# Retention attention with a SoLU layer: late transposes moved from TensorE to DMA, second-layer output in its own PSUM banks, more load buffers

## The chip, the core and the metric

The kernel runs on one core of a Trainium2 chip. The metric is the time of one execution on the device in microseconds (us). The engines that compute are TensorE (PE; its weight loads are shown as PEld), VectorE (DVE), ScalarE (ACT) and GpSimd (POOL); SyncE (SP) issues most of the transfers, which sixteen DMA engines carry out. SBUF is the working memory with 128 partitions; PSUM is the memory of eight banks into which TensorE writes.

## What is computed

The inputs are q, k and v of shape 8 x 8 x 576 x 64 (batch, head, position, feature), and a layer with w_in (512 x 1024), w_out (1024 x 512) and a gain g_ln (1024), all float32. The output has 4608 rows of 512.

```python
scores = np.matmul(q, k.transpose(0, 1, 3, 2)) / np.sqrt(D)
gamma = 1.0 - 2.0 ** (-5.0 - np.arange(H))
Dmat = np.where(rel >= 0, gamma[:, None, None] ** rel, 0.0)    # rel = row position - column position
x = np.matmul(scores * Dmat, v)                  # heads side by side: 4608 rows of 512
h = x @ w_in
e = np.exp(h - h.max(-1))
solu = h * e / e.sum(-1)
ln = (solu - mean(solu)) / np.sqrt(var(solu) + 1e-6) * g_ln
out = ln @ w_out
```

Retention (the first part) has no softmax, so it can be done in windows: inside a window by a masked score matrix, and from the windows before it by a running state of k-transposed times v.

## The kernel before

**Windows, steps and tiles.** The 576 positions of a batch element are cut into two windows of 256 and a rest of 64; the rests of four batch elements make one more window. That gives 18 windows, each done in two halves of four heads: 36 *steps* i of the attention. Each window also gives two blocks of 128 output rows: 36 *tiles* t of the layer.

**One step** consists of named operations, whose names with the number of the step or tile appear in the order lists and in the prediction:

- `ldq`, `ldk`, `ldv`: the loads into the pool `raw` (lines 375 to 385), five buffers of each kind.
- `sq`, `sk`, `cv`: scaling of q and k by powers of gamma, with a cast to 16 bits (L394), and the cast of v (L399), mostly on POOL. The 16-bit pools hold three q, four k and four v.
- `T`: q and k transposed on TensorE into PSUM, `qk_tp`. Before step 10 in 128x128 blocks (L419), from then on in quarters of 64x64 (L429).
- `K`: the product of k and v for the state (L472); `st` (DVE), `sm` and `sc` (POOL) scale the state and put it into block form (lines 543 to 571).
- `S`: the scores (L508) from the transposed q and k; `mask` multiplies them with the triangle (L540, DVE).
- `I` and `V`: the part of the output from the state, and the part from the masked scores (both L472), into the PSUM tile `xy`; `xe` copies it to the 16-bit `xT` (L576, ACT).

**One tile** consists of:

- `M1`: x times w_in into the two PSUM banks of `h` (L587); `ex`: exponential on ACT (L595); `so`: h times the exponential into `solu` (L605, L610, DVE), four buffers.
- `bnA`, `bnB`: statistics for the normalisation (L616, L618, DVE); for the first four tiles ACT does them (`va`). `fx`, `fin` and `rs` make the factor of a row (ACT, DVE, POOL). The mean is taken out beforehand, by centring the columns of w_out times g_ln (`wg`, `WM`, `wc`).
- `L`: `solu` transposed on TensorE, `ln_tp`, in 128x128 blocks for tiles 0 to 3 (L439), then in quarters (L446).
- `M2`: the second product (L660); `oe`: eviction with the factor of the row (L669, ACT) into `osb`, three buffers; `out`: the store.

**Joint transposes.** From step 10 on the transposes of step i and of tile i - 6 go into one PSUM tile `tl` (two banks), and one copy on ACT, `TL` (L457), brings both to one SBUF tile of the pool `ev`, which has eight buffers. Scores, the state product and M2 read it from there. The last six tiles' L's have a copy of their own, `Le`; the first steps use `Te` and `Le` with a tile of their own each (L455). `tl_of`, `tl_ev`, `ev_T` and `ev_L` arrange this.

**PSUM.** `xy`, `s` and `h` have two banks each, and the two banks of the first transposes (`tl1`) are later the two of `tl`. M2 writes into `s`, or, for odd tiles from 31 on, into `xy`; `late` tells which.

**The order.** `plan` lists every operation with its engine, a duration, the operations that it depends on, and the buffers that it takes and who releases them. A key places it in its engine's queue: the lists `FIRST` (the start) and `LAST` (the end) are written out by hand, and between them the key follows from the step's number times 4.92 us and an offset of the kind. `order_ops` runs this plan with its durations and gives each operation a start; the program is then recorded in that order, so each engine executes its queue strictly in order. All loads and stores except the last store stand in SP's queue. Each DMA, in both kernels, also waits for the one issued eight before it.

**Fillers.** Where the plan leaves TensorE without work ahead of the first M2, products of zeros are put in (L846).

After the main part a branch recomputes everything in a general way if a row's sum of exponentials lies outside a fixed range; with these inputs it isn't taken.

## Time and profile before

| | us |
|---|---|
| median of 3 runs | 213.56 |
| lowest and highest run | 212.74, 213.57 |
| span of the profiled execution, first to last instruction | 210.9 |
| PE busy in that span | 200.8 |
| DVE busy | 166.1 |
| ACT busy | 141.7 |
| POOL busy | 141.7 |

The page gives the profiled execution by its span; the runs' times also hold what lies before the first and behind the last instruction. Its mean granted TensorE clock is 0.999. The three product kinds L587, L660 and the transposes L446 and L429 are the rows of TensorE that the change concerns; their busy times are 68.5 us (288 instructions), 67.6 us (296), 14.2 us (1024) and 8.3 + 8.1 us (416 each). Small products in quarters of the array run beside each other, so busy times of neighbouring groups overlap, and the distance between the starts of two groups is what one of them takes of the queue. In a row of the timeline stand the start in us, the duration in us, engine, line, operation, output and input with their shapes, and the number of instructions; a bracket holds idle time just before it and what ended it. In a row of the stages stand the stretch, then each engine's busy time and count, the granted clock, the share of time that the DMA engines were busy, and GB/s.

### The profile page before, as it was taken

What the parts mean: (1) busy time and instruction counts of PE and PEld (TensorE: products, weight loads), DVE (VectorE), ACT (ScalarE), POOL (GpSimd) and SP (SyncE); (2) the same over time, 40 slices, a digit from 0 to 9 for tenths busy, and PEclk for the clock granted to TensorE, in tenths of its full rate; (3) what the DMA queues carried; (4) which work ended last, traced back from release to release, by engine and by line L of the source; (5) the groups of instructions that cost most, each with busy time, mean ns of one, the idle gap of its engine ahead of it and who ended that gap; (6) DMA issues with size and microseconds to landing.
All of it is one profiled execution on the core that took longest, in us unless ns stands there. A gap on an engine that the chain in (4) does not pass through costs nothing. (4 is left out here: it accounts for less than half of the span.)

```text
span 210.9 us, 10171 instructions
## 1 busy us (share of the span) xinstructions
PE 200.8 (95%) x4400; PEld 113.2 (54%) x4400; DVE 166.1 (79%) x279; ACT 141.7 (67%) x235; POOL 141.7 (67%) x240
## 2 busy tenths in 40 slices
PE   7986989999999999999999999999999999999992
PEld 2442654665566555555555555555666555554451
DVE  6565779997868898978898898889988998753760
ACT  2375787897666776776666777666767777573752
POOL 7434758999997975948787979797979792001110
PEclk9999999999999999999999999999999999999999
DMA  5999999999666559778999686776355222311224
GB/s 157 345 355 334 329 311 269 301 293 306 195 188 188 169 139 278 217 214 259 314 288 305 198 252 183 217 234 181 94 152 153 54 57 67 71 63 54 101 101 104
DMA packets 64814, 42.66 MB, mean 202 GB/s; under 512 B 3320, under 2 KB 58624, under 8 KB 64768
## 3 DMA queue, kind: packets, MB, share of 16 engines
q1 hardware_dynamic: 64528, 41.82, 68.4%
q8 instruction: 34, 0.56, 1.2%
q10 hardware_dynamic: 240, 0.18, 0.5%
q14 instruction: 12, 0.10, 0.2%
HBM read 32.55 MB, written 9.44 MB: 199 GB/s over the span
## 5 line engine op out<-in xcount | busy, mean ns | idle before, releaser
L587 PE MATMUL h_ps<-w_in,xT 128*128 128x512 f16 x288 | 68.5, 380 | 0.0
L660 PE MATMUL o_ps<-w2c,ev 128*128 128x512 f16 (+1 forms) x296 | 67.6, 373 | 0.0
L610 DVE TENSOR_TENSOR solu<-h_ps,e_sb 128x1024 f16<-128x1024 f32 x32 | 39.2, 1223 | 16.7 <-ACT e_sb L595 16.5
L595 ACT ACTIVATE e_sb<-h_ps 128x1024 f32<-128x1024 f32 x36 | 36.8, 1023 | 21.9 <-PE h_ps L587 20.4
L540 DVE TENSOR_TENSOR ret<-s_ps,masks 128x1024 f16<-128x1024 f32 x36 | 43.9, 1220 | 6.0 <-PE s_ps L508 5.4
L660 PEld LDWEIGHTS <-ev 128*128 128x128 f16 x296 | 28.7, 98 | 32.7
L616 DVE BATCH_NORM_STATS2 bs<-solu 128x6 f32<-128x512 f16 x64 | 43.6, 685 | 0.9
L587 PEld LDWEIGHTS <-xT 128*128 128x128 f16 x288 | 25.3, 98 | 29.1 <-ACT xT L576 0.8
L394 POOL TENSOR_TENSOR q<-rawq,small 128x512 f16<-128x512 f32 x34 | 35.4, 1042 | 7.3 <-DMA rawq<-in_q_dram 5.9
L669 ACT ACTIVATE o_sb<-o_ps,rs 128x512 f32<-128x512 f32 (+1 forms) x37 | 25.0, 676 | 21.8 <-PE o_ps L660 10.4
L394 POOL TENSOR_TENSOR k<-rawk,small 128x512 f16<-128x512 f32 x34 | 35.4, 1042 | 6.0 <-DMA rawk<-in_k_dram 5.9
L457 ACT COPY ev<-tl 128x1024 f32<-128x1024 f32 (+1 forms) x32 | 29.7, 932 | 4.7 <-PE tl L429 4.2
L576 ACT CAST xT<-xy 128x512 f16<-128x512 f32 x36 | 26.7, 742 | 3.0 <-PE xy L472 2.9
L571 POOL CAST sbd<-gg 64x256 f16<-64x256 f32 x64 | 25.4, 397 | 3.0
L562 POOL TENSOR_TENSOR gg<-gt,small 128x128 f32<-128x128 f32 x32 | 13.1, 409 | 16.9 <-DVE gt L557 16.5
L648 POOL TENSOR_TENSOR w<-mv,w 128x2 f32<-128x2 f32 x16 | 3.1, 194 | 27.8 <-ACT w L633 13.9
L399 POOL CAST v<-rawv 128x512 f16<-128x512 f32 x28 | 17.1, 609 | 0.2
L508 PE MATMUL s_ps<-ev 64*64 64x128 f16 x576 | 14.8, 218 | 0.3
L472 PE MATMUL xy<-ret,v 64*64 64x128 f16 x576 | 14.7, 217 | 0.0
L472 PEld LDWEIGHTS <-sbd 128*128 128x128 f16 x128 | 9.3, 98 | 9.3 <-issue 1.1
L446 PE MATMUL tl<-ident,solu 64*64 64x64 f16 x1024 | 14.2, 195 | 0.0
L846 PE MATMUL tl<-zeros 128*128 128x512 f16 x41 | 12.7, 445 | 1.3 <-DVE zeros L802 1.3
(71 smaller groups left out, 214.6 us busy)
## 6 DMA issues: line engine op xcount, KB each, us to landing
rawq<-in_q_dram SPq DMA_DIRECT2D x32, 256.0 KB, 5.1
rawk<-in_k_dram SPq DMA_DIRECT2D x32, 256.0 KB, 5.3
rawv<-in_v_dram SPq DMA_DIRECT2D x32, 256.0 KB, 5.1
out_dram<-o_sb SPq DMA_DIRECT2D x26, 256.0 KB, 3.1
out_dram<-o_sb SPq DMA_DIRECT2D x19, 128.0 KB, 2.3
wst<-in_moe_w_in_dram SPq DMA_DIRECT2D x4, 512.0 KB, 6.8
wst<-in_moe_w_out_dram SPq DMA_DIRECT2D x4, 512.0 KB, 7.1
rawq<-in_q_dram SPq DMA_DIRECT2D x16, 64.0 KB, 2.4
```

Of the source, the lines that this page charges most:

```text
L394: eng.tensor_tensor(out=t.rearrange("p j h d -> p h j d"), in0=st[i]["r" + nm], in1=g, op=ALU.mult)
L457: nc.scalar.copy(out=t[:, lo:hi].rearrange("p x (r w) -> p r x w", r=2), in_=tls[n].rearrange("p r x w -> p (r x w)").bitcast(FP).rearrang ...
L472: nc.tensor.matmul(start=(c, e) not in begun, stop=False, skip_group_check=True, **kw)
L540: nc.vector.tensor_tensor(out=d["ret"].rearrange("p e h j q -> p (e h) (j q)"), in0=d["s"].rearrange("p e h j q -> p (e h) (j q)"), in1=ma ...
L571: nc.gpsimd.tensor_copy(out=t[ee[e], :, :, ee[e]], in_=st[i]["gg"][ee[e]])
L576: nc.scalar.copy(out=xT[:, 2 * w : 2 * w + 2, 2 * hf : 2 * hf + 2].rearrange("p c h (q j) -> p c h j q", j=2), in_=xys[i][:, :, 0:256].rea ...
L587: nc.tensor.matmul(out=h_ps[:, hh], lhsT=xT[:, t, dc], rhs=w_in16[:, dc, hh], start=(dc == 0), stop=(dc == 3),)
L595: nc.scalar.activation(out=d["e"], in_=d["h"], func=ACT.Exp, accum_out=se[:, t : t + 1])
L610: nc.vector.tensor_tensor(out=d["solu"], in0=d["h"], in1=d["e"], op=ALU.mult)
L616: nc.vector.bn_stats(out=d["bs"][:, half], in_=d["solu"][:, half * 512 : half * 512 + 512])
L660: nc.tensor.matmul(out=o, lhsT=d["ev"][:, d["lo"] + c], rhs=w2c16[:, c, mm], start=(c == 0), stop=(c == 7))
L669: nc.scalar.activation(out=d["osb"][:, mm], in_=d["o", half], func=ACT.Copy, scale=ws[t // 2]["rs"][:, t % 2 : t % 2 + 1])
```

## The change

- **q and k by DMA.** For steps 28 to 35 (`TX`) the operation `T` and its copy are replaced by `tx`: two DMA transposes on SP's queue, from the 16-bit q and k in SBUF straight into an `ev` tile (`qk_dma`). The blocks lie in another order there, which `qk_of` takes into account.
- **The activation by DMA.** For tiles 20 to 33 (`LX`) `L` and its copy are replaced by `lx`: one DMA transpose of `solu` into an `ev` tile (`ln_dma`). T26 and T27 thereby lose their joint partner and get a copy `Te` of their own. L34 and L35 stay on TensorE, now in whole 128x128 blocks.
- **Own banks for M2.** From tile 20 (`OT`) on M2 writes into a pool `o2` of two banks, which are the banks of `tl`, closed after the last joint transpose; L34 and L35 use them too. M2_35 and its second half stay in `h` and `xy`.
- **More load buffers.** The pool `wst`, in which w_in and w_out are loaded, is closed after use, and in its place a pool `bis` with three buffers each of q, k and v is opened. The loads of the steps i >= 13 with (i - 13) mod 8 >= 5, that is 18 to 20, 26 to 28 and 34 to 35, go there.
- **The order of every operation** is written out in a list `ORDER`, for all engines from start to end; `FIRST` and `LAST` and the formula between them are gone. Work of an engine is otherwise the same, save for what is named above. In the built program TensorE has 3661 products in place of 4423, and 35 fillers in place of 45; SP has 30 transposes, 16 of 128x512 and 14 of 128x1024, each named with pieces of 16x128.

The diff, cut to this; of the order lists, the parts of TensorE and SP from step 25 on and DVE and POOL near the end:

```diff
-    ldx=0.88, ldw=1.36, out=0.65,
+    ldx=0.88, ldw=1.36, out=0.65, tx=1.0, lx=0.6, ltx=0.9,
...
-    rawq=5, rawk=5, rawv=5, q16=3, k16=4, v16=4, ev=8, s=1, ret=2, xy=1, gg=6, gt=2, s160=4, s161=9, h=1,
-    e=2, solu=4, osb=3, tl=1, tlx=2, tlT=1, tlL=1, wst=5,
+    rawq=5, rawk=5, rawv=5, bisq=3, bisk=3, bisv=3, q16=3, k16=4, v16=4, ev=8, s=1, ret=2, xy=1, gg=6, gt=2, s160=4, s161=9, h=1,
+    e=2, solu=4, osb=3, o2=2, tl=1, tlx=2, tlT=1, tlL=1, wst=5,
...
+LX = (20, 21, 22, 23, 24, 25, 26, 27, 28, 29, 30, 31, 32, 33)
+TX = (28, 29, 30, 31, 32, 33, 34, 35)
+R0 = 13
+OT = 20
+
+
+ORDER = dict(
...
+    PE=(
...
+        "M2_15 I22 L18 V22 T24 S23 K24 M1_20 M2_16 I23 V23 L19 K25 T25 S24 M1_21 M2_17 I24 T26 V24 K26 S25 M1_22 M2_18  "
+        "I25 T27 V25 K27 S26 M1_23 M2_19 I26 V26 K28 S27 M1_24 M2_20 I27 S28 V27 K29 M1_25 I28 V28 S29 K30 M2_21 M1_26  "
+        "I29 V29 S30 K31 M2_22 M1_27 I30 S31 V30 K32 M2_23 M1_28 I31 S32 V31 K33 M2_24 M1_29 I32 S33 V32 M2_25 M1_30 I33  "
+        "V33 S34 M2_26 M1_31 I34 S35 V34 M2_27 M1_32 I35 V35 M2_28 M1_33 M2_31 M2_29 M1_34 M2_30 M2_32 M1_35 M2_33 L34  "
         "L35 cs M2_34 M2_35 M3"
...
+    DVE=(
...
+        "bnA21 mask25 bnB20 st26 so22 bnA22 mask26 bnB21 st27 so23 bnB22 st28 mask27 bnA23 so24 mask28 st29 bnB23 bnA24  "
+        "so25 st30 mask29 bnA25 so26 st31 mask30 bnB24 so27 st32 mask31 bnB25 so28 st33 mask32 bnA26 bnA27 so29 mask33  "
+        "bnB27 bnB26 so30 mask34 bnA29 bnB29 so31 mask35 bnA28 bnB28 so32 bnA30 bnA31 bnB31 bnB30 so33 bnA32 bnA33 bnB32  "
+        "bnB33 so34 bnA34 bnB34 so35 cnt bnA35 bnB35 ci"
...
+    POOL=(
...
+        "cv26 sq25 rs8 sc23 sm24 sq28 cv27 sk27 sk29 sc24 rs9 sm25 cv28 sq27 sc25 sk30 sq29 sm26 sq31 sc26 cv29 sm27  "
+        "sc27 sm28 cv31 rs10 sc28 sq30 cv30 sm29 sk31 sc29 cv32 sk32 sm30 cv33 rs11 sq32 sc30 sm31 sc31 sq35 sk33 sq33  "
+        "sk34 sq34 sm32 sc32 rs12 cv34 sm33 sk35 sc33 cv35 rs13 rs14 rs15 rs16 rs17"
...
+    SP=(
...
+        "ldv25 ldk30 ldq25 out12 ldk27 ldv31 ldk29 out11 ldq29 ldv26 ldq31 ldk34 ldv30 out14 ldv29 out13 ldv27 ldq27  "
+        "ldq30 out15 ldq35 ldk35 ldk33 tx28 ldk31 out16 ldk32 ldv33 lx20 tx29 ldv32 out17 lx21 ldv34 lx22 ldq32 tx30  "
+        "out18 out20 ldq34 tx31 lx24 out19 lx23 ldv35 lx26 lx25 tx32 ldq33 out21 out22 tx33 tx34 lx27 lx29 tx35 lx28  "
+        "out23 out24 out26 out25 lx31 lx30 out27 out28 lx32 lx33 out31 out29 out32 out33 out30 out34 out35"
...
-    return f"Te{i}" if i < NJ + 2 else f"TL{i - 2}"
+    return f"tx{i}" if i in TX else f"Te{i}" if i < NJ + 2 or i - 6 in LX else f"TL{i - 2}"
...
-    return f"Le{t}" if t < NJ - 4 or t + 4 > NS - 3 else f"TL{t + 4}"
+    return f"lx{t}" if t in LX else f"Le{t}" if t < NJ - 4 or t + 6 >= NS or t + 6 in TX else f"TL{t + 4}"
+
+
+def extra(i):
+    return i >= R0 and (i - R0) % 8 >= 5
+
+
+def home(t):
+    return "h" if t == NT - 1 else "o2" if t >= OT else "xy" if late(t) and t % 2 else "s"
 
...
-    return name[0] == "T" and int(name[1:]) < NJ + 2 or name[0] == "L" and int(name[1:]) < NJ - 4
+    return name[0] == "T" and int(name[1:]) < NJ + 2 or name[0] == "L" and (int(name[1:]) < NJ - 4 or int(name[1:]) >= OT)
...
-        jn = i >= NJ + 2
-        op(f"T{i}", "PE", "T" if jn else "Tw", [f"sq{i}", f"sk{i}", f"L{i - 6}" if jn else ""], (n, 0.4), [] if jn else [("tlT", [f"Te{i}"])])
-        if jn:
-            op(f"TL{n}", "ACT", "TL", [f"T{i}", f"L{i - 6}"], (n, 1.0), [("ev", [f"I{i}", f"S{i}", f"M2_{i - 6}"])])
-        else:
-            op(f"Te{i}", "ACT", "Te", [f"T{i}"], (n, 1.0), [("ev", [f"I{i}", f"S{i}"])])
+        jn, alone = i >= NJ + 2, i - 6 in LX
+        if i in TX:
+            op(f"tx{i}", "SP", "tx", [f"sq{i}", f"sk{i}"], (n, 0.4), [("ev", [f"I{i}", f"S{i}"])], DUR["ltx"])
+        else:
+            op(f"T{i}", "PE", "T" if jn else "Tw", [f"sq{i}", f"sk{i}", f"L{i - 6}" if jn and not alone else ""], (n, 0.4),
+               ([("tl", [f"Te{i}"])] if alone else []) if jn else [("tlT", [f"Te{i}"])])
+            if jn and not alone:
+                op(f"TL{n}", "ACT", "TL", [f"T{i}", f"L{i - 6}"], (n, 1.0), [("ev", [f"I{i}", f"S{i}", f"M2_{i - 6}"])])
+            else:
+                op(f"Te{i}", "ACT", "Te", [f"T{i}"], (n, 1.0), [("ev", [f"I{i}", f"S{i}"])])
         op(f"S{i}", "PE", "S", [ev_T(i)], (i - 1, 0.95), [("s", [f"mask{i}"])])
...
-        op(f"so{t}", "DVE", "soA" if va else "so", [f"ex{t}"], (m, 4.56), [("solu", [f"L{t}", f"va{t}" if va else f"bnB{t}"])])
+        op(f"so{t}", "DVE", "soA" if va else "so", [f"ex{t}"], (m, 4.56), [("solu", [f"lx{t}" if t in LX else f"L{t}", f"va{t}" if va else f"bnB{t}"])])
...
+        if t in LX:
+            op(f"lx{t}", "SP", "lx", [f"so{t}"], (m + 2, 0.1), [("ev", [f"M2_{t}"])], DUR["ltx"])
+        lasts = [x for x in range(NT) if NJ - 4 <= x < OT and ev_L(x)[:2] == "Le"]
+        after = [f"Te{NJ + 1}", f"Le{NJ - 5}"] if t == NJ - 4 else []
+        if t in lasts:
+            after += [f"Le{t - 2}" if t - 2 in lasts else ev_T(max(i for i in range(NS) if i not in TX))]
+        if t not in LX:
+            op(f"L{t}", "PE", "Lw" if wide(f"L{t}") else "L", [f"so{t}"] + after, (m + 2, 0.1),
+               [("tlL" if early else "o2" if t >= OT else "tl" if jn else "tlx", [ev_L(t)])])
+        if ev_L(t)[:2] == "Le":
             op(f"Le{t}", "ACT", "Le", [f"L{t}"], (m + 2, 0.95), [("ev", [f"M2_{t}", "M3" if t == NT - 1 else ""])])
...
+        if t == OT:
+            need += [ev_T(min(TX) - 1), ev_L(max(x for x in range(NT) if x not in LX and x < min(LX)))]
+        op(f"M2_{t}", "PE", "M2h" if end else "M2", need, (t + LAG, 3.1), [(home(t), [f"oe{t}"])])
...
-        st[i]["r" + nm] = t = pools["raw"].tile([P, 4, 2, D], FP, tag=nm, name="raw" + nm)
+        if extra(i) and "bis" not in pools:
+            loads_w.close()
+            pool("bis", CAP["bisq"])
+        st[i]["r" + nm] = t = pools["bis" if extra(i) else "raw"].tile([P, 4, 2, D], FP, tag=nm, name="raw" + nm)
...
+    def bank():
+        if "o2" not in pools:
+            banks_2.close()
+            pool("o2", CAP["o2"], space=PS)
+        return pools["o2"].tile([P, 512], FP, tag="o2", name="o_ps")
...
-                pool("tl", 1, space=PS)
+                pools["tl"] = banks_2.enter_context(tc.tile_pool(name="tl", bufs=1, space=PS))
+                ctx.callback(banks_2.close)
...
-            x = tl1[1].rearrange("p (x w) -> p x w", w=P)
+            if t >= OT:
+                tk[t]["tl"] = bank().bitcast(F16)
+            x = (tk[t]["tl"] if t >= OT else tl1[1]).rearrange("p (x w) -> p x w", w=P)
...
+    def blocks():
+        t = pools["ev"].tile([P, 16, 64], FP, tag="ev", name="ev")
+        return t.rearrange("p x w -> p (x w)").bitcast(F16).rearrange("p (x w) -> p x w", w=P)[:, 0:8]
+
+    def qk_dma(i):
+        st[i]["ev"] = t = blocks()
+        for n, nm in enumerate(("q16", "k16")):
+            nc.sync.dma_start_transpose(out=t[:, 4 * n : 4 * n + 4], in_=st[i][nm].rearrange("p j h d -> p (j h d)"))
+
+    def ln_dma(t):
+        tk[t]["lo"] = 0
+        tk[t]["ev"] = x = blocks()
+        nc.sync.dma_start_transpose(out=x, in_=tk[t]["solu"])
+
     def qk_of(i, n):
-        return st[i]["ev"][:, 4 * n : 4 * n + 4].rearrange("p (h j) w -> p h j w", j=2)
+        x = st[i]["ev"][:, 4 * n : 4 * n + 4]
+        return x.rearrange("p (j h) w -> p h j w", j=2) if i in TX else x.rearrange("p (h j) w -> p h j w", j=2)
...
-        nm = "h" if t == NT - 1 and not half else nm
+        nm = "xy" if half else home(t)
         mm = slice(256 * half, 256 * half + (256 if t == NT - 1 else DM))
-        d["o", half] = o = pools[nm].tile([P, 2, 512], FP, tag=nm, name="o_ps")[:, 0, 0 : mm.stop - mm.start]
+        o = bank() if nm == "o2" else pools[nm].tile([P, 2, 512], FP, tag=nm, name="o_ps")[:, 0]
+        d["o", half] = o = o[:, 0 : mm.stop - mm.start]
```

More of the change, by code (lines that the diff above doesn't have):

```diff
@@ L36 @@
 CAP = dict(
-    rawq=5, rawk=5, rawv=5, q16=3, k16=4, v16=4, ev=8, s=1, ret=2, xy=1, gg=6, gt=2, s160=4, s161=9, h=1,
-    e=2, solu=4, osb=3, tl=1, tlx=2, tlT=1, tlL=1, wst=5,
-)
-FIRST = dict(
-    PE=(
[5 rows of a table removed]
-    ),
-    ACT=(
[4 rows of a table removed]
-    ),
-    DVE=(
[5 rows of a table removed]
-    ),
-    POOL=(
[4 rows of a table removed]
-    ),
-    SP=(
[5 rows of a table removed]
-    ),
-)
-LAST = dict(
-    PE=(
-        "I34 L30 V34 S35 M1_32 I35 L31 V35 M2_28 M1_33 M2_29 M2_31 M1_34 L32 M2_30 L33 L34 M1_35 M2_32 M2_33 "
+    rawq=5, rawk=5, rawv=5, bisq=3, bisk=3, bisv=3, q16=3, k16=4, v16=4, ev=8, s=1, ret=2, xy=1, gg=6, gt=2, s160=4, s161=9, h=1,
+    e=2, solu=4, osb=3, o2=2, tl=1, tlx=2, tlT=1, tlL=1, wst=5,
+)
+LX = (20, 21, 22, 23, 24, 25, 26, 27, 28, 29, 30, 31, 32, 33)
[3 more added lines that the diff above has]
+ORDER = dict(
+    PE=(
[10 rows of a table added]
         "L35 cs M2_34 M2_35 M3"
@@ L339 @@
     pool("raw", CAP["rawq"])
-    for name in ("q16", "k16", "v16", "ev", "ret", "gg", "gt", "e", "solu", "osb", "wst"):
+    for name in ("q16", "k16", "v16", "ev", "ret", "gg", "gt", "e", "solu", "osb"):
         pool(name, CAP[name])
@@ L867 @@
                 emit(o)
+    if "bis" not in pools:
+        loads_w.close()
+    pool("gu", 1)
     def general(t):
```

45 lines of the change are left out of this document (21 added, 24 removed), and 53 rows, old and new, of tables (ACT, DVE, PE, POOL).

## The prediction, made before the result was known

> **What bounds the kernel now.** I read the engine shares first, then the slices, then the busy time by stage.
>
> ```profile
> span 210.9 us, 10171 instructions
> PE 200.8 (95%) x4400; PEld 113.2 (54%) x4400; DVE 166.1 (79%) x279; ACT 141.7 (67%) x235; POOL 141.7 (67%) x240
> PE   7986989999999999999999999999999999999992
> DMA  5999999999666559778999686776355222311224
> core 0: us, PE busy (x) PEld busy (x) DVE busy (x) ACT busy (x) POOL busy (x), PEclk, DMA share, GB/s
> 120.00:140.00 20.00, 20.00 (x527) 11.56 (x526) 18.05 (x29) 14.16 (x23) 17.03 (x29) 1.00 0.76 214
> 140.00:160.00 20.00, 20.00 (x527) 11.55 (x526) 18.07 (x30) 14.01 (x23) 17.04 (x30) 1.00 0.51 145
> 160.00:180.00 20.00, 20.00 (x496) 11.38 (x495) 17.74 (x27) 13.93 (x22) 13.62 (x23) 1.00 0.35 86
> 180.00:200.00 20.00, 20.00 (x302) 10.15 (x300) 12.05 (x19) 12.18 (x22) 1.72 (x4) 1.00 0.20 67
> ```
>
> TensorE is busy in all of 120 to 200 us, so there the end moves by what leaves its queue, as long as its operands come in time. DVE has some 2 us spare in 20 up to 180 us, then 8. The DMA engines are full early and at 0.2 to 0.5 late: room for the new transfers lies where the change puts them. A busy PE need not be at its peak, so I price its work by distances between starts, in one step of the steady stage:
>
> ```profile
> 138.85 1.90 PE L587 MATMUL h_ps<-w_in,xT 128*128 128x512 f16 x8
> 140.59 1.89 PE L660 MATMUL o_ps<-w2c,ev 128*128 128x512 f16 x8
> 142.31 0.27 PE L472 MATMUL xy<-ev,sbd 128*128 128x128 f16 x2
> 142.52 0.45 PE L446 MATMUL tl<-ident,solu 64*64 64x64 f16 x32
> 142.79 0.30 PE L429 MATMUL tl<-ident,q 64*64 64x64 f16 x16
> 142.92 0.31 PE L429 MATMUL tl<-ident,k 64*64 64x64 f16 x16
> 143.05 0.41 PE L472 MATMUL xy<-ret,v 64*64 64x128 f16 x16
> 143.27 0.31 PE L472 MATMUL xy<-v,k 64*64 64x64 f16 x16
> 143.40 0.41 PE L508 MATMUL s_ps<-ev 64*64 64x128 f16 x16
> 143.74 1.47 PE L587 MATMUL h_ps<-w_in,xT 128*128 128x512 f16 x6
> ```
>
> In order: M1, M2, I, L, T (q, k), V, K, S, next M1. L takes 142.79 - 142.52 = 0.27 us, T 143.05 - 142.79 = 0.26, and the step 143.74 - 138.85 = 4.89. The busy figures (0.45; 0.30 + 0.31) overlap their neighbours and would overstate what is saved.
>
> **TensorE, removed and added.** T28 to T35 go: 8 x 0.26 = 2.1 us. L20 to L31 go from steps of this kind: 12 x 0.27 = 3.2. The last L's stand in the tail:
>
> ```profile
> 194.31 0.45 PE L446 MATMUL tl<-ident,solu 64*64 64x64 f16 x32
> 194.69 1.90 PE L660 MATMUL o_ps<-w2c,ev 128*128 128x512 f16 x8
> 196.52 0.77 PE L446 MATMUL tl<-ident,solu 64*64 64x64 f16 x64
> 197.22 1.90 PE L587 MATMUL h_ps<-w_in,xT 128*128 128x512 f16 x8
> 24.82 0.62 PE L439 MATMUL tl<-ident,solu 128*128 128x128 f16 x8
> 25.28 0.59 PE L846 MATMUL tl<-zeros 128*128 128x512 f16 x2
> 45.25 1.89 PE L660 MATMUL o_ps<-w2c,ev 128*128 128x512 f16 x8
> ```
>
> L32 is 0.38, L33 half of the pair's 0.70 = 0.35; together 0.7. L34 and L35 stay, as eight whole 128x128 blocks: 25.28 - 24.82 = 0.46 each in place of 0.35, so +0.2. Removed 2.1 + 3.2 + 0.7 = 6.0; net 5.8.
>
> One wait is new. In the new order M2_32 stands before M1_35, and only M2_33 and L34 lie between M1_35 and L35, which needs so35. Rows for such a chain, and for the state chain used below:
>
> ```profile
> 160.37 1.89 PE L660 MATMUL o_ps<-w2c,ev 128*128 128x512 f16 x8
> 160.56 1.02 ACT L595 ACTIVATE e_sb<-h_ps 128x1024 f32<-128x1024 f32 x1 [0.72 <-PE h_ps L587]
> 161.71 1.23 DVE L610 TENSOR_TENSOR solu<-h_ps,e_sb 128x1024 f16<-128x1024 f32 x1 [0.31 <-ACT e_sb L595]
> 164.83 0.29 DVE L556 TENSOR_TENSOR gg<-xy,gg 128x128 f32<-128x128 f32 x1
> 165.53 0.40 POOL L562 TENSOR_TENSOR gg<-gt,small 128x128 f32<-128x128 f32 x1 [0.92 <-DVE gt L557]
> 165.99 0.83 POOL L571 CAST sbd<-gg 64x256 f16<-64x256 f32 x2
> 167.83 1.04 POOL L394 TENSOR_TENSOR q<-rawq,small 128x512 f16<-128x512 f32 x1
> L669 ACT ACTIVATE o_sb<-o_ps,rs 128x512 f32<-128x512 f32 (+1 forms) x37 | 25.0, 676 | 21.8 <-PE o_ps L660 10.4
> ```
>
> From the end of M1's slot (160.37, where M2 starts) to the end of the product is 161.71 + 1.23 - 160.37 = 2.57 us. M2 (140.59 to 142.31, 1.72) and L34 (0.46) cover 2.18, so L35 waits 0.4. Net gain 5.8 - 0.4 = 5.4 us.
>
> **Can the other engines follow the shorter step?** Without L and T the step is 4.89 - 0.53 = 4.36 us. The single h buffer needs M1 (1.74), then 2.57 until the product is done: 4.31, which just fits. DVE's 18.07 us in 20 is 4.42 per 4.89 us step, just over 4.36; the new order moves some statistics (bnA, bnB) behind the last masks, into the 8 us free after 180. If that cover were gone, six steps would cost 0.1 more each. POOL at 17.04 in 20 needs 4.17 and fits. ACT loses copies (ten joint ones, two halves) and is bound nowhere. The two own banks for M2 (o2) keep S from waiting for the eviction once T and L no longer stand between; without them that would be up to the eviction's 0.68 a step (the row of L669). I cost these at nothing, with 1 us of loss as an end.
>
> **The transposes' price** stands in no row. The nearest are plain transfers and SP's issues:
>
> ```profile
> rawq<-in_q_dram SPq DMA_DIRECT2D x32, 256.0 KB, 5.1
> out_dram<-o_sb SPq DMA_DIRECT2D x19, 128.0 KB, 2.3
> 139.23 0.67 SPq L379 DMA_DIRECT2D rawq<-in_q_dram  x1
> 123.45 0.36 SPq L680 DMA_DIRECT2D out_dram<-o_sb  x1
> 146.26 3.15 SPq L384 DMA_DIRECT2D rawk<-in_k_dram  x4
> ```
>
> So one issue takes 0.36 to 0.79 us of SP (3.15 / 4), and data land 2.3 to 5.1 us after it. A tx (two issues) then takes 0.7 + 2.3 = 3.0 us at best and 1.6 + 5.1 = 6.7 at worst; I take 4.5, as the sizes lie with the small store and the DMA engines are half idle by then. An activation tile lies between 2.7 and 5.9. Most of its users stand two steps or more behind their so; the closest is M2_31, put ahead of M2_29: from M1_31 to it lie M2_27, M2_28, M1_32, M1_33 and the small work of I34 to V35, 2 x 1.72 + 2 x 1.74 + 1.3 = 8.2 us, less so31's 2.57 a lead of 5.6.
>
> The tightest lead is S33. In POOL's new order sk33 and sq33 follow sc31, which hangs on K31 and so26. Counted from the end of M1_26: so26 2.57; st31 to sc31 165.99 + 0.83 - 164.83 = 2.0; sq35, sk33, sq33 3 x 1.0; together 7.6 us. TensorE reaches S33 after three steps of 4.36 and I32 (0.2), 13.3. The lead is 5.7: fine at 4.5, 1.0 late at 6.7. A late tx33 would hold V33, M1_30 and all of TensorE's queue behind S33, and on SP tx34, lx27 and the stores behind it. All 8 ev tiles would be in use there (a tx and an lx each step, where one joint tile served both), so a late M2 also makes the next tx late.
>
> SP itself: tx28 stands after out15, issued at 123.45, so the stretch runs from about 126 us to some 190, when lx33 is due (M2_33 follows M1_35, at 197.22 before). Between them stand 30 transposes and 39 copies. The copies take 39 x 0.5 = 20 us and leave 44 us, 2.0 us for each of the 22 tiles (8 tx, 14 lx). By the rows a tile needs 30/22 x 0.79 = 1.1 at most. SP keeps up.
>
> On this point the Trainium skill has two rules. Its page "Advanced Engine Details and Errata", section "X-Bar Transpose (TRN2)", has such DMAs "as fast as regular DMAs", and by it the sum above stays. "VectorE: DVE Perf Modes", section "The three transpose paths", gives 1309 ns for one 128x128 block by DMA against 390 ns on TensorE; eight blocks one after another would be 10.5 us by my estimate, five times what SP's stretch has for a tile. No run here shows either yet.
>
> **The front.** All other orders are written anew, and the loads of steps 18 to 20, 26 to 28, 34 and 35 have three buffers of each kind of their own. The work is the same. The built program has 35 filling matmuls where the old had 45: its plan sees smaller gaps ahead of the first M2. Bounds from the waits on POOL and DMA of that stage (the first two digits of PE's slices, and the zeros that fill it): 2 us better to 2 us worse; I take 0.
>
> Sum: 210.9 - 5.4 = 205.5 us of span. The profiled execution's own time is shown by its span alone; the median 213.56 lies 2.66 above it, so 208.2 us. I forecast **208.2 us**, with its own range 206 to 211 (front -2 to +2, followers up to 1 us).
>
> **Rivals.**
> Late operands (0.15): transposes share the DMA engines with loads that now run further ahead and land 7 to 8 us after their wait ends, so S33 and its neighbours stall some 2.3 us, once, since the following leads grow by it. For it: the lead of 5.7 and the full ev pool. Against: a DMA share of 0.35 after 160 us. 208.2 + 2.3 = 210.5.
>
> SP's queue becomes the bound (0.29): the other side. A transpose tile occupies the queue, or the one stream behind it, for more than 2.0 us; from there each 0.1 us costs 22 x 0.1 = 2.2 us, because stores, last loads and later tiles stand in the same order behind it. At 2.4 us a tile: 208.2 + 22 x 0.4 = 217. It eats the whole gain at 2.25 us. For it: the built instruction cuts a tile into 64 pieces of 16x128, and no row prices those. Against: no issue of a load takes more than 0.79. The 1309 ns a block of the Trainium skill's page "VectorE: DVE Perf Modes" would be this rival far past its point; I hold that alone at 0.04, inside the 0.29.
>
> The new order ahead of step 28 loses what the end gains (0.11): loads for later tiles (ldq18 before ldq12) go ahead of nearer ones while the DMA slices are at 9, POOL waits, and TensorE shows gaps in 20 to 120 us where it had none. 4 to 6 us of such gaps give 212 to 214; 213 in the middle.
>
> That DVE or the h loop holds the step at 4.5 costs 6 x 0.14 = 0.8 and stays inside the forecast's range.
>
> **Numbers.** Forecast 0.45, late 0.15, SP 0.29, front 0.11. This kernel's measurement can tell 0.5%, 1.1 us, from no change. Faster takes the forecast (0.44), most of late (0.11) and a little of SP and front (0.02): 0.57. Same: 0.09 from the edges. Slower: most of SP and half of front, 0.34. The range reaches from 205.5 (front better by 2, followers free) to 220 (2.55 us a tile), leaving out the worse SP cases.
>
> **What would show it.** Right: 576 and 512 small transposes left (T10 to T27, L4 to L19), steps of 4.4 us after step 28, no PE wait on ev, transposes landing within 5 us, L35 waiting 0.4. Late: PE waits on the DMA of ev at L508 or L660. SP: its transposes' issues above 2 us a tile, stores late, ACT waiting for o_sb. Front: PE slices under 9 before 120 us with waits on POOL or raw loads. The forecast is wrong if a tx takes over 6 us from wait to landing, or the first M2 (45.25 above) starts 3 us later.

## The result, and the profile after

| | before | after |
|---|---|---|
| median | 213.44 us (4 runs on the same chip) | 231.79 us (231.02 to 233.53, 4 runs) |
| after to before | | 1.088 (95% interval 1.083 to 1.093) |
| span of the profiled execution | 210.9 us | 229.7 us |

The changed kernel is 18.35 us slower; 208.2 us was forecast, with 206 to 211 as its own range and 205.5 to 220 with the rivals. Some executions of any of these kernels run some per cent longer than its others, TensorE at a lower clock; ratios leave those out, and where only two runs of a kernel exist, both are given.

The engine shares, the slices and the transfer queue of the page of after, and the queue of before, which the prediction did not show (packets, MB, share of the time of 16 DMA engines):

```profile
span 229.7 us, 8648 instructions
PE 199.9 (87%) x3638; PEld 110.0 (48%) x3638; DVE 162.6 (71%) x279; ACT 130.0 (57%) x223; POOL 141.3 (61%) x240
PE   7699888999599997699999999997759599969990
q1 hardware_dynamic: 88016, 47.60, 79.4%
```

```profile
q1 hardware_dynamic: 64528, 41.82, 68.4%
```

Before had nothing but nines from slice 7 up to the last; now there are holes at slices 11, 16 and 17, and from 28 on at 28 to 30, 32 and 36. By stage (busy time of each engine in 20 us, then granted clock and DMA share):

```profile
40.00:60.00 20.00, 17.37 (x362) 10.66 (x359) 14.66 (x25) 13.48 (x24) 18.53 (x29) 1.00 0.99 261
60.00:80.00 20.00, 19.65 (x496) 11.42 (x498) 16.09 (x27) 13.56 (x23) 13.46 (x23) 1.00 0.72 204
80.00:100.00 20.00, 15.90 (x452) 9.35 (x444) 13.00 (x19) 10.76 (x17) 12.14 (x21) 1.00 0.70 204
...
140.00:160.00 20.00, 18.38 (x339) 10.09 (x329) 16.20 (x28) 10.94 (x20) 16.61 (x30) 1.00 0.98 173
160.00:180.00 20.00, 14.15 (x147) 6.74 (x144) 10.69 (x18) 6.04 (x12) 6.95 (x13) 0.83 0.73 171
180.00:200.00 20.00, 18.78 (x222) 9.34 (x223) 13.89 (x20) 8.35 (x15) 9.23 (x16) 0.91 0.72 143
200.00:220.00 20.00, 17.62 (x107) 8.13 (x105) 12.88 (x23) 10.06 (x21) 2.66 (x6) 1.00 0.65 149
```

There are two losses. **The front:** TensorE idles 2.63 + 0.35 + 4.10 = 7.1 us between 40 and 100, and M2_19 starts 6.3 us late (146.93 against 140.59). The first M2 is still on time (45.17 against 45.25), so the prediction's sign for the front, a first M2 3 us late, could not show this loss. **The tail:** from M2_19 to the end it is 229.7 - 146.93 = 82.8 us against 70.3 before, +12.5 in place of the -5.4 that was forecast, 17.9 worse. TensorE idles 1.6 + 5.9 + 1.2 + 2.4 = 11.1 us there; the granted clock of 0.83 and 0.91 takes, by estimate, at most 0.17 x 20 + 0.09 x 20 = 5.2 more.

**What the front waits for.** One GpSimd row with its wait, SP's issues of that load (four, for a rest window), what TensorE waited for, and M2_19 (start, length, engine, line, operation; in brackets the idle time ahead and what ended it):

```profile
83.74 2.10 SPq L421 DMA_DIRECT2D rawk<-in_k_dram  x4
89.81 1.04 POOL L431 TENSOR_TENSOR k<-rawk,small 128x512 f16<-128x512 f32 x1 [7.41 <-DMA rawk<-in_k_dram]
92.72 0.29 PE L533 MATMUL xy<-ev,sbd 128*128 128x128 f16 x2 [1.86 <-POOL sbd L632]
146.93 1.89 PE L721 MATMUL o_ps<-w2c,ev 128*128 128x512 f16 x8
```

By GpSimd's order this is k of step 17. Its load stands in SP's new order behind ldq18, ldq20, ldk23, ldv22, ldv24 and others for later steps.

**What the tail waits for.** First SP's price of a transpose, from the views of its two lines and of a store's (smallest, median, largest ns; first and last start):

```profile
L516 SPq DMA_TRANSPOSE ev<-q x8: 1200/1206/2105, 139.4 to 191.7; - x8
L516 SPq DMA_TRANSPOSE ev<-k x8: 1207/1257/1903, 140.8 to 193.9; - x8
DMA to landing us min/median/max: 2.4/2.5/4.3
L521 SPq DMA_TRANSPOSE ev<-solu x14: 1232/1284/3038, 146.0 to 209.8; - x14
DMA to landing us min/median/max: 3.1/3.2/5.4
L741 SPq DMA_DIRECT2D out_dram<-o_sb x38: 332/480/1473, 47.9 to 220.5; - x38
```

A transposing issue holds SP for 1.2 us or more, a store for 0.48; 128x512 and 128x1024 cost it nearly the same. By the medians the 22 tiles take 8 x 1.206 + 8 x 1.257 + 14 x 1.284 = 37.7 us of SP, 1.71 each. (In the changed kernel's plan stand 0.6 us for an activation and 1.0 us for q and k together: `lx=0.6`, `tx=1.0`.) Then a stretch of SP's queue, and how a late store becomes a hole of TensorE:

```profile
157.44 1.26 SPq L521 DMA_TRANSPOSE ev<-solu  x1
158.75 0.61 SPq L416 DMA_DIRECT2D rawq<-in_q_dram  x1
159.47 1.20 SPq L516 DMA_TRANSPOSE ev<-q  x1
160.72 1.26 SPq L516 DMA_TRANSPOSE ev<-k  x1
162.08 1.00 SPq L741 DMA_DIRECT2D out_dram<-o_sb  x2
163.13 2.92 SPq L421 DMA_DIRECT2D rawq<-in_q_dram  x4
166.32 0.69 ACT L730 ACTIVATE o_sb<-o_ps,rs 128x512 f32<-128x512 f32 x1 [6.20 <-DMA out_dram<-o_sb]
167.00 1.01 ACT L656 ACTIVATE e_sb<-h_ps 128x1024 f32<-128x1024 f32 x1
168.13 1.23 DVE L671 TENSOR_TENSOR solu<-h_ps,e_sb 128x1024 f16<-128x1024 f32 x1 [5.30 <-ACT e_sb L656]
169.41 3.57 PE L648 MATMUL h_ps<-w_in,xT 128*128 128x512 f16 x8 [3.78 <-DVE solu L671]
```

SP goes from issue to issue with no gap to speak of. The two stores at 162.08 are those of tiles 18 and 20. Tile 18's eviction ended at 144.79; since the store ahead of it (152.35) SP had issued four transposes and five parts of loads, in the order of its list. Until these stores land ScalarE has no free `o_sb`. So it waits 6.2 us in its eviction, the exponential is queued behind it, VectorE's product behind that, and M1, which needs `h` free, stands 3.78 us. The next eight matmuls take 3.57 us in place of 1.90, at a granted clock of 0.50 (stretches of 1 us, 168 to 174 us).

The other large holes of the tail are waits for operands that came late: 1.22 us ahead of M2_21 (158.56), 2.41 ahead of S32 (180.68) and 2.15 ahead of M2_31 (207.11). Their transposes were issued late: tile 21's at 153.58, where its activation was ready at 139.43; step 32's from 176.89 on, where its q and k were ready at 169.14; tile 31's at 203.70, where its activation was ready at 198.49, behind eight parts of stores that SP issued from 196.56 on.

### The profile page after: what moved, and what is told of

Same layout as the page of the kernel before. It is cut to its first block, busy times and chain, and to the rows that moved or that the text cites. A ratio compares the mean times of both kernels' runs of the same rounds, so it can differ in the third digit from the quotient of the medians.

```text
span 229.7 us, 8648 instructions
## 1 busy us (share of the span) xinstructions
PE 199.9 (87%) x3638; PEld 110.0 (48%) x3638; DVE 162.6 (71%) x279; ACT 130.0 (57%) x223; POOL 141.3 (61%) x240
## 5 line engine op out<-in xcount | busy, mean ns | idle before, releaser
L648 PE MATMUL h_ps<-w_in,xT 128*128 128x512 f16 x288 | 70.2, 387 | 3.9 <-DVE solu L671 3.8
L721 PE MATMUL o_ps<-w2c,ev 128*128 128x512 f16 (+1 forms) x296 | 69.4, 380 | 3.4 <-DMA ev<-solu 3.4
L648 PEld LDWEIGHTS <-xT 128*128 128x128 f16 x288 | 26.6, 99 | 35.6 <-issue 7.2
L677 DVE BATCH_NORM_STATS2 bs<-solu 128x6 f32<-128x512 f16 x64 | 42.5, 679 | 0.2
L503 ACT COPY ev<-tl 128x1024 f32<-128x1024 f32 (+1 forms) x18 | 17.4, 965 | 4.2 <-PE tl L473 4.1
L569 PE MATMUL s_ps<-ev 64*64 64x128 f16 x576 | 15.4, 225 | 4.8 <-DMA ev<-k 2.9
L533 PE MATMUL xy<-ev,sbd 128*128 128x128 f16 (+1 forms) x128 | 12.8, 214 | 2.7 <-POOL sbd L632 2.5
L569 PEld LDWEIGHTS <-ev 64*64 64x64 f16 x576 | 10.2, 109 | 7.9 <-DMA ev<-k 3.6
```

The costliest lines, as they stand in the source:

```text
L533: nc.tensor.matmul(start=(c, e) not in begun, stop=False, skip_group_check=True, **kw)
L569: nc.tensor.matmul(out=sv[ee[c], e, hp, j], lhsT=kT[ee[e], hp, j, ee[c]], rhs=qT[ee[e], hp, :, ee[c]], start=True, stop=True,)
L648: nc.tensor.matmul(out=h_ps[:, hh], lhsT=xT[:, t, dc], rhs=w_in16[:, dc, hh], start=(dc == 0), stop=(dc == 3),)
L677: nc.vector.bn_stats(out=d["bs"][:, half], in_=d["solu"][:, half * 512 : half * 512 + 512])
L721: nc.tensor.matmul(out=o, lhsT=d["ev"][:, d["lo"] + c], rhs=w2c16[:, c, mm], start=(c == 0), stop=(c == 7))
```

## The experiments

Theory A: the tail is lost because each transposing issue takes SP 1.25 us, whatever its size, in a queue that also carries the stores and the last loads; the front is lost by the new order of the loads. The other letters are explained where they are used.

**Old orders to the front, the new tail kept** (`e1_front_old`). All five orders of before to about 104 us, then those of after.

```diff
 ORDER = dict(
     SP=(
-        "ldk0 ldv0 ldq0 ldq1 ldk1 ldv1 lwi0 lwi3 lwi1 lwi2 ldq2 ldv2 ldk2 ldk3 ldq3 ldv3 lwo4 lwo0 ldk4 ldv4 ldq4 lwo6  "
+        "ldq0 ldk0 ldv0 ldv1 ldq1 ldk1 lwi1 lwi2 lwi0 lwi3 ldk2 ldv2 ldq2 ldk3 ldq3 ldv3 lwo4 lwo0 ldk4 ldq4 ldv4 lwo6 "
...
```

> The changed kernel with the old queue orders of all engines up to about 104 us and the new ones from there on; transposes and banks as changed. The changed kernel's trace has M2_19 6.3 us late (146.93 against 140.59) before any transpose by DMA is waited for, and from M2_19 to the end 82.8 us against 70.3. Theory A (two separate losses: the new early order costs 6 us; SP's queue is too slow for the transposes, 1.25 us an issue): M2_19 near 141 to 142, the rest still 8 to 13 us longer than before, time 222 to 226. Rival C (the late stalls exist only because the queues' orders were planned for an earlier arrival): with M2_19 on time the rest takes 65 to 70 us, time 207 to 213.

Measured: 230.65 us (ratio 1.081, 1.071 to 1.090). The holes between 40 and 100 us shrink to 0.5 us, and M2_19 starts at 144.14, of whose delay M2_0 has 2.45 already (47.70 against 45.25). The tail takes 228.7 - 144.14 = 84.6 us, no better than 82.8. The time lies outside both expectations: the front came back by 2.8 us only, and the tail grew by 1.8. Still, with M2_19 2.8 us earlier the tail is no shorter, so it does not lose its time because the front is late.

**The new front, the old tail** (`e2_front_new`). The new orders and load buffers to about 124 us; no transposes by DMA.

```diff
-LX = (20, 21, 22, 23, 24, 25, 26, 27, 28, 29, 30, 31, 32, 33)
-TX = (28, 29, 30, 31, 32, 33, 34, 35)
+LX = ()
+TX = ()
...
-OT = 20
+OT = 99
```

> The complement: new queue orders and load buffers up to about 124 us, then the old order; no transpose by DMA, no own banks for M2. Theory A: the front's loss alone, 213.4 + 6 = 218 to 220, with waits of POOL for raw q and k between 55 and 95 us and TensorE gaps of 2.7, 1.2, 1.9 and 1.2 us there. Rival (the early gaps are a chance of one run, or are taken up again later): 213 to 215.

Measured: 219.54 and 223.69 us. By the faster of the two runs the front costs 6.1 us by itself.

**One k moved in SP's order** (`e5_k17_early`). The kernel of `e2_front_new`, with

```diff
-        ... ldv14 ldk15 out1 ldk19 ldk16 ldk23 "
-        "out2 out3 ldv15 ldv19 ldk18 ldq17 ldq15 ldv17 ldq23 ldv22 ldv16 ldq21 ldv18 ldv20 out4 ldk20 out5 ldv24 ldk17 "
+        ... ldv14 ldk15 out1 ldk19 ldk16 ldk17 "
+        "ldk23 out2 out3 ldv15 ldv19 ldk18 ldq17 ldq15 ldv17 ldq23 ldv22 ldv16 ldq21 ldv18 ldv20 out4 ldk20 out5 ldv24 "
```

> The kernel of e2_front_new (new queue orders and load buffers to about 124 us, no transposes by DMA) with one load moved: k of step 17 is issued where k of step 23 stood, eight SP entries earlier, and k of step 23 right behind it. Theory A's front term (the stall of POOL on rawk, 7.4 us from 82.4 in the profile of after, is that one load, issued behind twelve loads for later steps): most of TensorE's gaps between 85 and 95 go, 4 to 5 us less than the 219.5 of e2's better time: 214.5 to 216. Rival (the new orders of the engines themselves lose the time, with the load only the last to come): within 1.5 us of 219.5.

Measured: 218.63 us (ratio 1.020, 1.008 to 1.033). A miss, inside the rival's range (within 1.5 us of 219.5): the wait on rawk is gone, but another late tile takes its place,

```profile
74.96 0.61 POOL L435 CAST v<-rawv 128x512 f16<-128x512 f32 x1 [5.18 <-DMA rawv<-in_v_dram]
```

so it isn't this one load. Whether it is the order of the loads as a whole or the engines' own new orders, the next run tells.

**Only SP's order put back** (`e10_old_loads`). The kernel of `e2_front_new` with the SP list of before; the four other engines keep the new orders.

```diff
     SP=(
-        "ldk0 ldv0 ldq0 ldq1 ldk1 ldv1 lwi0 lwi3 lwi1 lwi2 ldq2 ldv2 ldk2 ldk3 ldq3 ldv3 lwo4 lwo0 ldk4 ldv4 ldq4 lwo6 "
...
+        "ldq0 ldk0 ldv0 ldv1 ldq1 ldk1 lwi1 lwi2 lwi0 lwi3 ldk2 ldv2 ldq2 ldk3 ldq3 ldv3 lwo4 lwo0 ldk4 ldq4 ldv4 lwo6 "
...
```

> The kernel of e2_front_new with the whole SP queue (loads and stores) put back into the order of before; TensorE, ScalarE, VectorE and GpSimd keep the new orders to about 124 us. If the loads' order is what the front loses: 213 to 215.5, no wait of GpSimd on a raw tile over 3 us after 50 us. Rival (the new orders of the engines lose it themselves, with any load order): 217.5 or more, with waits on raw tiles still there.

Measured: 213.15 us (ratio 0.998, 0.994 to 1.003), and by stage, as above:

```profile
40.00:60.00 20.00, 19.22 (x459) 12.02 (x457) 15.93 (x27) 14.93 (x27) 19.29 (x30) 1.00 0.92 260
60.00:80.00 20.00, 20.00 (x525) 11.76 (x526) 17.25 (x29) 13.74 (x24) 16.56 (x28) 1.00 0.61 177
80.00:100.00 20.00, 20.00 (x506) 11.75 (x505) 16.47 (x25) 13.99 (x23) 15.72 (x25) 1.00 0.83 245
```

One wait of GpSimd on a raw tile, 3.29 us at 88.83, is a little over the 3 us of the expectation, and it costs TensorE nothing. The whole loss of the front is SP's order, which up to there is mostly loads; the new orders of the engines lose nothing measurable.

**Eight issues fewer** (`e3_merged`). The changed kernel with the scaled q and k of steps 28 to 35 in one tile, transposed at once: the same bytes, 22 issues in place of 30.

```diff
+            if "qk16" not in pools:
+                pool("qk16", 4)
...
-        for n, nm in enumerate(("q16", "k16")):
-            nc.sync.dma_start_transpose(out=t[:, 4 * n : 4 * n + 4], in_=st[i][nm].rearrange("p j h d -> p (j h d)"))
+        nc.sync.dma_start_transpose(out=t, in_=st[i]["qk"].rearrange("p x j h d -> p (x j h d)"))
```

> The changed kernel with scaled q and k of steps 28 to 35 in one tile, so that one transpose of 128x1024 takes the place of two of 128x512; eight issues fewer. Theory A (the price is SP's time per issue, 1.21 us for 128x512 and 1.28 for 128x1024): SP saves 8 x 1.2 = 10 us between 139 and 196 us, the late stalls shrink by 5 to 10 us, time 222 to 227. Rival B (landing or the DMA engines set the pace): the same bytes, no gain, 230 to 233.

Measured: 220.11 and 225.06 us, 7 to 12 less than after. The view of its line, and the queue:

```profile
L522 SPq DMA_TRANSPOSE ev<-qk x8: 1231/1261/3038, 141.1 to 185.9; - x8
q1 hardware_dynamic: 87760, 47.59, 82.0%
```

Twice the width costs SP hardly more per issue (1.261 against 1.206 and 1.257). The DMA engines' time has not fallen (0.820 x 223.2 = 183.0 us, after 0.794 x 229.7 = 182.4), so the gain is not the traffic's. The joint tiles have a pool of their own with four buffers, in place of three of q and four of k that the other steps use too; in after no wait of GpSimd behind 140 us is put down to a transpose that still reads q or k, so these buffers are not a likely cause, but they were not tried alone.

**Stores issued by ScalarE** (`e4_stores_act`). The changed kernel with the stores of tiles 18 to 34 in ScalarE's queue, behind their eviction.

```diff
-                nc.sync.dma_start(out=out[r0 + r : r0 + r + n, :], in_=tk[t]["osb"][r : r + n])
+                (nc.scalar if t >= 18 else nc.sync).dma_start(out=out[r0 + r : r0 + r + n, :], in_=tk[t]["osb"][r : r + n])
...
-                q_dma = nc.scalar if t == NT - 1 and r else nc.sync
+                q_dma = nc.scalar if t == NT - 1 and r or 18 <= t < NT - 1 else nc.sync
```

> The changed kernel with the stores of tiles 18 to 35 issued from ScalarE's queue right behind their eviction. Theory A: SP loses some 25 issues of 0.57 us, 14 us, and the evictions no longer wait for stores that stand behind transposes (11.6 us of ScalarE's waits, one of 6.2 us that stopped TensorE for 3.8): time 219 to 225, TensorE gaps over 2 us gone. Rival B (landing or the DMA engines): 229 to 233. If ScalarE's issues hold up its exponentials, 225 to 230 with its waits at L656.

Measured: 237.67 us (ratio 1.114, 1.103 to 1.124), slower than after. As the program has it, a transfer waits for the one issued eight before it, on whatever queue that was. On ScalarE this wait now stands in the way of computation:

```profile
149.55 0.37 ACTq L741 DMA_DIRECT2D out_dram<-o_sb  x1
149.96 0.73 ACT L637 CAST xT<-xy 128x512 f16<-128x512 f32 x1 [5.51 <-DMA rawk<-in_k_dram]
```

The run moved the wait into a worse queue and tells nothing about SP's price.

**Transposes that nobody waits for** (`e6_idle_transposes`). Orders and work of before; 30 transposes of a constant are added to SP's queue, at the times at which the real ones' data are ready in before.

```diff
+    def idle_dma(n):
...
+        for x in range(n):
+            w = 1024 // n
+            t = pools["scr"].tile([P, 8 // n, P], F16, tag=f"scr{n}", name="scr")
+            nc.sync.dma_start_transpose(out=t, in_=w_in16[:, 0, w * x : w * x + w])
```

> The orders of before, all transposes on TensorE as before, and 30 DMA transposes added on SP's queue that read a constant and that nobody waits for: 14 of 128x1024 and 16 of 128x512, at the times where the data of the real ones are ready in before (134 to 195 us). Theory A (SP's time per issue is the cost, 30 x 1.25 = 38 us): SP is full from 134 on, loads of steps 31 to 35 and stores are late, ACT waits for o_sb: 214.5 to 219. Rival B (what costs is that operands come by DMA, late by issue plus landing, and that SP stands waiting for them in order): nothing here waits, so 213 to 214. Rival D (the transposes' traffic slows the loads): loads land later than their 5.1 us median, without a gap-free SP.

Measured: 228.06 us (ratio 1.065, 1.057 to 1.074): 14 us lost though no operand comes by a transpose. So the loss does not need operands that come late by DMA (rival B): a full SP queue alone can cost as much. TensorE's two largest holes, 3.95 us (ended at 169.28) and 5.07 (at 182.36), end with an eviction of ScalarE that had waited for a store. The loss is more than theory A had expected (to 219), and the price of an issue is higher than in after where several stand together (three from 181.12 on take 5.08 us):

```profile
L553 SPq DMA_TRANSPOSE scr<-w_in x30: 1189/1354/2853, 131.0 to 213.6; - x30
```

**The same bytes in 11 issues** (`e9_idle_half`).

```diff
-        for x in range(n):
-            w = 1024 // n
-            t = pools["scr"].tile([P, 8 // n, P], F16, tag=f"scr{n}", name="scr")
-            nc.sync.dma_start_transpose(out=t, in_=w_in16[:, 0, w * x : w * x + w])
+        t = pools["scr"].tile([P, 16, P], F16, tag="scr", name="scr")
+        nc.sync.dma_start_transpose(out=t, in_=w_in16[:, 0:2, :].rearrange("p c f -> p (c f)"))
```

> The kernel of e6_idle_transposes (orders and work of before, transposes that nobody waits for) with the same bytes in 11 transposes of 128x2048 in place of 14 of 128x1024 and 16 of 128x512, at every second of the same places in SP's queue. Theory A (SP's time per issue, some 1.25 us whatever the size): 11 x 1.3 = 14 us of SP in place of 38, so most of e6's loss goes: 213 to 217. Rival D (the traffic of the transposes, which is the same): as e6_idle_transposes, 226 to 229. If a 128x2048 issue takes 2.5 us or more, the price goes by size and theory A's fixed price falls.

Measured: 221.61 us (ratio 1.037, 1.027 to 1.047), between the two. The price, and the stall that remains:

```profile
L540 SPq DMA_TRANSPOSE scr<-w_in x11: 1584/2993/4452, 130.7 to 194.5; - x11
165.69 0.69 ACT L749 ACTIVATE o_sb<-o_ps,rs 128x512 f32<-128x512 f32 x1 [3.27 <-DMA out_dram<-o_sb]
166.42 0.42 PE L588 MATMUL s_ps<-ev 64*64 64x128 f16 x16 [2.33 <-ACT o_sb L749]
```

It is the chain of after: a store late behind SP's transposes, ScalarE without `o_sb`, TensorE behind it (here at the scores, which share a bank with M2's output). A 128x2048 issue takes 1.58 us at its best and 3.0 in the median, so a price that is fixed whatever the size holds only to 128x1024; at 128x2048, by the expectation's own condition (2.5 us or more), it falls. Rival D, the traffic, does not account for the loss alone: the same bytes lose 6 us less. The loss falls with SP's time, by the medians about 30 x 1.354 = 41 us for 14 us lost and 11 x 2.993 = 33 us for 8; these are two points and no law, and what the traffic adds to SP's time at this size was not separated.

**Only the activation by DMA, in the orders of before** (`e7_lx_only`). M2 has no banks of its own here; the load buffers of after stay.

```diff
-LX = ()
+LX = (20, 21, 22, 23, 24, 25, 26, 27, 28, 29, 30, 31, 32, 33)
```

> The orders of before; only the activation of tiles 20 to 33 goes by DMA (14 transposes of 128x1024, each in SP's queue where its product is ready), q and k stay on TensorE, no own banks for the second layer. TensorE loses 14 x 0.27 = 3.8 us of work. Theory A: 14 x 1.25 = 17.5 us of SP fit beside the last loads and the stores, so most of it is gained: 210 to 212. Rival B (operands by DMA come late, whatever SP's load): waits of M2 on the DMA of ev, 214 or more.

Measured: 213.82 us (ratio 1.004, 0.997 to 1.010; ten runs, from 212.99 to 217.35). A miss by some 2 us or more, for two reasons. One store is late again:

```profile
143.94 1.90 PE L649 MATMUL h_ps<-w_in,xT 128*128 128x512 f16 x8
148.74 1.90 PE L649 MATMUL h_ps<-w_in,xT 128*128 128x512 f16 x8
...
168.57 0.69 ACT L731 ACTIVATE o_sb<-o_ps,rs 128x512 f32<-128x512 f32 x1 [2.47 <-DMA out_dram<-o_sb]
169.31 0.42 PE L570 MATMUL s_ps<-ev 64*64 64x128 f16 x16 [1.79 <-ACT o_sb L731]
```

And a step is 148.74 - 143.94 = 4.80 us long, often 4.75, where 4.89 less 0.27 would be 4.62. In this kernel M2 still writes into the bank of the scores; whether that is what holds the step was not tried alone.

**Only q and k by DMA, in the orders of before** (`e8_tx_only`). Again without own banks for M2.

```diff
-TX = ()
+TX = (28, 29, 30, 31, 32, 33, 34, 35)
```

> The orders of before; only q and k of steps 28 to 35 go by DMA (16 transposes of 128x512), the activation stays on TensorE, no own banks for the second layer. TensorE loses 8 x 0.26 = 2.1 us. Theory A: 16 x 1.25 = 20 us of SP between 139 and 178, in which SP still issues the loads of steps 31 to 35 (some 24 issues) and eight stores: it is about full until 160, so 212 to 217 with waits at the score matmuls. Rival B (lateness by landing alone): each of the eight waits about the same at the score matmul, up to the end.

Measured: 220.58 us (ratio 1.033, 1.025 to 1.041), beyond the range. It has one hole, not eight equal ones, so lateness by landing alone isn't it:

```profile
161.72 0.64 PE L570 MATMUL s_ps<-ev 64*64 64x128 f16 x16 [3.76 <-DMA ev<-k]
```

The q and k of step 30 are ready at 150.2 us; SP issues their transposes at 157.96 and 159.25, behind twelve parts of loads (of steps 34 and 35) and a store. The landing takes 2.5 us of the 11.5, the queue the rest. The granted clock in the 10 us around the hole is 0.66, by estimate another 3.4 us.

**The tail ordered again with the measured price** (`e11_replanned`, `e12_lx_replanned`). Orders of before to 118 us; behind it they were sought again with 1.4 and 1.8 us of SP for a transpose. `e12_lx_replanned` is `e7_lx_only` so ordered; `e11_replanned` has besides:

```diff
-TX = ()
+TX = (30, 31, 32, 33, 34, 35)
...
-OT = 99
+OT = 22
...
-        for n, nm in enumerate(("q16", "k16")):
-            nc.sync.dma_start_transpose(out=t[:, 4 * n : 4 * n + 4], in_=st[i][nm].rearrange("p j h d -> p (j h d)"))
+        nc.sync.dma_start_transpose(out=t, in_=st[i]["qk"].rearrange("p x j h d -> p (x j h d)"))
```

> A version that theory A calls for: the orders of before to 118 us; the activation of tiles 20 to 33 by DMA (14 issues), q and k of steps 30 to 35 in one tile and one transpose each (6 issues), own banks for the second layer from tile 22; the orders behind 118 us sought again with 1.4 and 1.8 us of SP for each transpose. TensorE loses 14 x 0.27 + 6 x 0.26 = 5.3 us of work, but steps with only one of the two gone measured 4.78 in place of 4.93 us. Theory A (SP's room is all that was missing): 210 to 213. Rival B (operands by DMA cost more than SP's time, through late landing and a full ev pool): 214 to 219.

> The kernel of e7_lx_only (activation of tiles 20 to 33 by DMA, q and k on TensorE) with the orders behind 118 us sought again with 1.4 and 1.8 us of SP for each transpose, so that no store stands behind the last loads. Theory A: e7's stall of 1.79 us at 169.31 behind a late store goes: 211 to 213. Rival (steps do not get shorter than 4.78 and another wait comes in its place): 213.5 to 216.

Measured: 213.65 us (ratio 0.999, 0.994 to 1.004) and 213.68 us (ratio 1.000, 0.997 to 1.003). The 18 us are gone in both, with 20 and 14 transposing issues in place of 30, and the front of before; no eviction of ScalarE behind 130 us waits for a store. Neither gains: `e12_lx_replanned` lies in its rival's range, `e11_replanned` between the two. In `e12_lx_replanned` TensorE has no hole over 0.74 us left behind 130 us, but its steps from 144 to 183 us are still 4.75 to 4.81 us long. In `e11_replanned` VectorE's product waits for the buffer out of which a transpose still reads, and M1 behind it:

```profile
182.70 1.23 DVE L678 TENSOR_TENSOR solu<-h_ps,e_sb 128x1024 f16<-128x1024 f32 x1 [2.34 <-DMA ev<-solu]
183.98 1.89 PE L655 MATMUL h_ps<-w_in,xT 128*128 128x512 f16 x8 [2.48 <-DVE solu L678]
```

**More buffers for what a transpose reads** (`e13_more_buffers`).

```diff
-    ... bisq=3, bisk=3, bisv=3, ...
-    e=2, solu=4, ...
+    ... bisq=2, bisk=2, bisv=2, ...
+    e=2, solu=6, ...
...
-                pool("qk16", 4)
+                pool("qk16", 5)
```

> The kernel of e11_replanned with six buffers for the activation in place of four and five for the joint q and k tile in place of four (paid for by two in place of three of the own load buffers), and the orders behind 118 us sought again with them. If what is left of e11's loss is that a tile which a DMA transposes stays taken until the transpose has landed (VectorE's product waited 2.34 us and TensorE 2.48 us behind it, GpSimd 3.8 us for the q and k tile): 209.5 to 212. If those waits only move on (to the transposes' operands, stores or raw tiles): 212.5 to 215, as before.

Measured: 211.17 us (12 runs; ratio 0.991, 0.988 to 0.994). This version is faster than after, and 0.9% below before: little, but the interval leaves out 1. No wait of VectorE on a transpose is left in its profile, and TensorE's longest behind the product is 0.73 us. Its orders were sought again with the buffers, so how much is the buffers' alone wasn't tried.

## Why the prediction was wrong

**TensorE's saving was right, where both transposes go.** Two M1's of the changed kernel, ahead of the tail's first hole, and its L35:

```profile
150.16 1.90 PE L648 MATMUL h_ps<-w_in,xT 128*128 128x512 f16 x8
154.52 1.69 PE L648 MATMUL h_ps<-w_in,xT 128*128 128x512 f16 x7
...
220.15 0.61 PE L485 MATMUL o_ps<-ident,solu 128*128 128x128 f16 x8 [0.33 <-DVE ca L801]
```

The step is 4.36 us, as forecast, and in `e11_replanned` three in a row are 4.35 or 4.36 (M1 at 164.58, 168.94, 173.29 and 177.65), so VectorE and the h loop can follow. With one of the two left it is longer than the sum has it: 4.75 to 4.80 without M2's own banks (`e7_lx_only`, `e8_tx_only`), and 4.80 in the changed kernel where T27 stays (M1 at 140.39 and 145.19). So steps 26 and 27, where only L goes, were not worth their full 0.27. The new wait in front of L35, forecast at 0.4, is 0.33 us.

**The landing was right.** Counted from the start of an issue, 3.2 us for the activation lies inside the allowed 2.7 to 5.9, and for q and k the first issue and the second's landing, 1.2 + 2.5 = 3.7, inside 3.0 to 6.7. The largest landings (5.4, and 2.1 + 4.3 = 6.4 at most) do too. Late operands end some of TensorE's waits, but because their issue was late, as shown above.

**The step that failed is "By the rows a tile needs 30/22 x 0.79 = 1.1 at most. SP keeps up."** It measured 1.71 us at the medians. The dearest copy was taken as the upper bound of an operation that no row priced, and that bound was then used as if it were known. The break-even of 2.0 us a tile was wrong as well: it spread SP's room from 126 to 190 us, but tx28 was issued at 139.44, and at 138.68 in `e1_front_old`. The store ahead of it in the list, out15, came at 132.79 in place of 123.45, and between the two stand nine parts of loads, which take SP from 133.65 to 139.34 and which the stretch left out. With 13.4 us less room the same sum gives (44 - 13.4) / 22 = 1.39; if the end moves out by the front's 6.3 us as well, 1.68. 1.71 is over both. And a mean does not show that a store ready at 144.79 is issued at 162.08, behind the transposes ahead of it in the list, and that with only three `o_sb` ScalarE then stands 6.2 us. The rival had the mechanism (stores late behind the transposes) and gave it 0.29; its point and size were off.

**The front was taken at 0 and measured 6.3 us.** "The work is the same" was true, and `e10_old_loads` shows that the engines' new orders cost nothing; the loads of later steps ahead of nearer ones do. The rival had this with 4 to 6 us at a chance of 0.11, as an alternative. It came together with the other one.

Added up, as an estimate: 213.4 - 5.4 (TensorE) + 6.3 (front) + 14.1 (30 issues that nobody waits for) = 228.4 of the 231.8 measured. This checks the size only. In the changed kernel's own trace the late store takes 3.78 us of TensorE and, with the clock at 0.50 behind it, an estimated 2.7 more; the three late operands take 5.78 and an estimated 1.7 of slow clock (181 to 185 us). That is 14.0 of the 17.9 that the tail lost, in about equal parts, both by SP's late issues; the rest was not resolved.

Of the two pages of the Trainium skill, "Advanced Engine Details and Errata", section "X-Bar Transpose (TRN2)" ("as fast as regular DMAs"), agrees in the landing (2.5 to 3.2 us against 2.3 to 5.1 of copies), not in the DMA engines' time (below); of SP's issue, 1.2 us against 0.48 here, that section says nothing. The 1309 ns for a 128x128 block of "VectorE: DVE Perf Modes", section "The three transpose paths", cannot be added up: eight blocks in one transfer landed in 3.2 us.

## What to carry to other kernels

A transfer that replaces an engine's work costs its issuing queue too: before moving dozens of them, get one measured issue price, and sum the queue's time in the stretch where they stand, from the time at which the queue gets there. Then look at what stands in order behind them (here the stores, and through `o_sb` ScalarE, VectorE and TensorE) and at which buffers they hold until they land. A new order of loads is a change of its own, and is tried alone.
